# Slot writes of a gated mixture rounded one by one, its last 32 slots of an expert in plain float32 on column groups, and a rounds loop inside a branch

## The chip, the cores and the metric

One core of a Trainium2 chip runs the whole program. The metric is the device time of one execution in microseconds (us). TensorE (PE) does the matmuls, its weight loads are listed apart (PEld), VectorE is DVE, ScalarE is ACT, GpSimd is POOL, and SyncE (SP) issues most of the direct DMAs. POOL issues the indirect DMAs, which gather or scatter rows by a list of indices.

## The reference, cut to what matters

```python
def _attn_ref(r, k, v, w, u):            # B, H, S, D = 4, 8, 768, 48
    for t in range(S):
        cur = einsum('bhd,bhe->bhde', u * kt, vt)
        y[:, :, t] = einsum('bhd,bhde->bhe', rt, state + cur)
        state = wt[..., None] * state + einsum('bhd,bhe->bhde', kt, vt)

def _moe_ref(x, w1, w2, w3, w_out):      # x 3072 x 384, d_ff 1024
    return ((x @ w1) * (x @ w2) @ w3) @ w_out

def _moe2_ref(x, w_gate, w_noise, noise, w1, w2):   # 8 experts, 384 -> 1024 -> 384
    noisy = x @ w_gate + log1p(exp(x @ w_noise)) * noise
    top2 = argpartition(-noisy, 2, axis=1)[:, :2]   # softmax over the two gives top2_w
    for e in range(8):
        for k in range(2):
            mask = top2[:, k] == e
            h = maximum(x[mask] @ w1[e], 0.0)
            out[mask] += top2_w[mask, k, None] * (h @ w2[e])
```

The three run one behind the other on 3072 rows: a linear attention, a gated product with folded weights, and a mixture of 8 experts of which every row takes two.

## The kernel before, in words

**Arithmetic.** A float32 product is made of three passes: each operand is split into a high and a low part (tiles that end in h and l, type fp32r), and `mm3` (lines 170 to 172) multiplies high by high, low by high and high by low into one PSUM bank.

**First part.** After w3 and w_out are folded into the other weights, twelve groups g of 256 rows run through attention and the first mixture. A group is 12 slots of PE work (`SPG = 12`, about 2.85 us a slot), and a table `todo` hangs the other steps on slots. Two of the slots of a group carry the output of an attention chunk: line 302, 56 short float32 matmuls (32 in one chunk of four or so) with 32 columns of weights each, on the four column groups of the array in turn. ACT and DVE split its result (L308, L309).

**Gate.** For four chunks of 128 rows at a time `gate_top` finds on DVE each row's two experts, their weights (`g_sc`) and the slot of each in a table in memory (`g_sf`, float32); L623 casts all 128x8 slots to int32 (`g_si`). `gate_put` writes one column of 128 table entries of 8 bytes by an indirect DMA from POOL (L640); eight of them make a gate group. `gate_at` hangs them on slots: groups 1 to 4 on (13, 14, 17, 17, 19, 20, 23, 23) counted from the gate's own group, the fifth (`late`) on (8, 9, 9, 11, 11, 13, 13, 13). DVE keeps the order in which the program is written; the other engines are put in order by the scheduler. The sixth and last gate group is computed within the first expert's `mm1(0, ff)`, and its eight puts are written behind that loop.

**Second part.** Eight experts have 800 slots each: six tiles of 128 rows and one of 32 (`TPL`), in two halves (4 tiles, then 2 and the 32 rows). For an expert SP loads the indices from the table (`load_idx`, `ti`), POOL gathers its rows (L722, `xg`), `tr` transposes them on PE (L731), `mm1(hf, ff)` makes eight strips of the hidden rows, ACT takes their ReLU (L744), DVE the low part (L746, L748), and `mm2(e, j)` makes a tile of output, scaled by the gate weight (L762) and added to the output by a scatter from POOL (L771). The last tile (j = NT - 1, L767) multiplies a 64-column weight, 32 high and 32 low columns beside each other (`HM`), by the high and the low half of w2: 16 matmuls. L769 and L770 add its two halves. Weights come as raw float32 (`raw`, `load_e`, two loads of 768 KB for each of w1 and w2) and are split ahead of time (`split_e`; L696 ACT for the high part, L701 POOL or DVE for the low part).

**Rounds.** Should an expert get more rows than it has slots, a loop at the end, `tc.For_i(1, n)`, runs experts again. With these inputs n is 1, and its body is not run.

Of the kernel before, what the change touches and what calls it, by code (L numbers as in the profile page):

```python
# [18 lines left out]
P = 128  # L19
# [52 lines left out]
def tile_kernel(ctx: ExitStack, tc: tile.TileContext, dt, nat, w3t, wout, w1, w2, e1, e2, cf, ci, out):  # L72
# [8 lines left out]
    def f(ap):  # L81
        return ap.bitcast(F32)
# [463 lines left out]
    def gate_top(t0, n):  # L546
        def gt(shape, name, dtp=F32, bufs=1):
            return gp.tile(shape, dtp, name=name, bufs=bufs)
# [68 lines left out]
                          in1=b2[:, None, :].to_broadcast([P, n, E]), op=OP.add)  # L617
        for k in range(2):
            dve.tensor_tensor(out=M[:, :, k], in0=M[:, :, k], in1=rb, op=OP.mult)
        sf = gt([P, n, 2], "g_sf")  # L620
        dve.tensor_reduce(out=sf, in_=M, axis=mybir.AxisListType.X, op=OP.add)
        si = gt([P, n, 2], "g_si", I32, 2)
        dve.tensor_copy(out=si, in_=sf)  # L623
        GT[t0] = (si, SC)
        yield
        if last and RMAX > 1:

# [8 lines left out]
            dve.tensor_copy(out=rounds, in_=rs)  # L636

    def gate_put(t0, i, k):
        si, SC = GT[t0]
        ins = pool.indirect_dma_start(out=table, out_offset=bass.IndirectOffsetOnAxis(ap=si[:, i, k:k + 1], axis=0),  # L640
                                      in_=SC[:, i, k, :], in_offset=None)
        for p in PUT:
            tc.declare_no_dep(ins.ins, p, reason="every slot is given once")
        PUT.append(ins.ins)
# [30 lines left out]
    def open_h(pl, hf):  # L675

        n = (TA, TB)[hf] * TPT
        HH[hf] = pl.tile([P, 8, 2 * NAB[hf]], F32R, name=f"HH{hf}")
        Hh[hf], HM[hf] = HH[hf][:, :, :NAB[hf]], HH[hf][:, :, n:2 * NAB[hf] - n]
        Hl[hf] = HH[hf][:, :, 2 * NAB[hf] - n:]  # L680

    def open_b():
        EP["b"] = ctx.enter_context(tc.tile_pool(name="epb", bufs=1, side="right"))
        open_h(EP["b"], 1)

    def load_e(e, m, i):
        rw = rawp.tile([P, 1538], F32, name="raw2", tag="raw64")[:, :1536]
        sp.dma_start(out=rw, in_=(e1, e2)[m][e, :, 1536 * i:1536 * i + 1536])
        RW[e, m, i] = rw

    def split_e(e, m, i, on=pool):
        s = slice(768 * i, 768 * i + 768)
        o = 768 * (i % 2)
        src = RW[e, m, i // 2][:, o:o + 768]
        h, l = (WAh, WBh)[m][:, s], (WAl, WBl)[m][:, s]
        cast = act.copy(out=h, in_=src)  # L696
        if e == 1:

            tc.keep_in_program_order(cast)
            on = dve  # L700
        on.tensor_tensor(out=l, in0=src, in1=f(h), op=OP.subtract)  # L701
# [35 lines left out]
    def mm1(hf, ff):  # L737
        n = NAB[hf]
        s0 = hf * NAB[0]
        bank = MB[ff % (2 + hf)][:, :n]  # L740
        for kb in range(3):
            w = slice(kb * FF + ff * P, kb * FF + ff * P + P)
            mm3(bank, WAh[:, w], WAl[:, w], XT["h"][:, kb, s0:s0 + n], XT["l"][:, kb, s0:s0 + n], kb == 0, kb == 2)
        act.activation(out=Hh[hf][:, ff], in_=bank, func=AF.Relu)  # L744
        n = (TA, TB)[hf] * TPT
        dve.scalar_tensor_tensor(Hl[hf][:, ff], bank[:, :n], 0.0, f(Hh[hf][:, ff, :n]), op0=OP.max, op1=OP.subtract)  # L746
        if hf == 1:
            dve.scalar_tensor_tensor(HM[hf][:, ff, TPL:], bank[:, n:], 0.0, f(HM[hf][:, ff, :TPL]),  # L748
                                     op0=OP.max, op1=OP.subtract)

    def mm2(e, j):
        hf, jj = divmod(j, TA)
        n, s = rows_of(j), slice(TPT * jj, TPT * jj + rows_of(j))
        MC[0] ^= 1
        bank = bX[MC[0]][:, :DM]
        y = EP["a"].tile([P, DM], F32, name="ye", bufs=3)
        wt = ti(e, j)[:, 1:2].bitcast(F32)
        if j < NT - 1:
            for ff in range(8):
                w = slice(ff * DM, ff * DM + DM)  # L760
                mm3(bank[:n], Hh[hf][:, ff, s], Hl[hf][:, ff, s], WBh[:, w], WBl[:, w], ff == 0, ff == 7)
            act.activation(out=y[:n], in_=bank[:n], func=AF.Copy, scale=wt)  # L762
        else:

            for ff in range(8):
                for i, ws in enumerate((WBh, WBl)):
                    pe.matmul(bank[:2 * n], HM[hf][:, ff], ws[:, ff * DM:ff * DM + DM],  # L767
                              start=ff == 0 and i == 0, stop=ff == 7 and i == 1)
            act.activation(out=y[:n], in_=bank[:n], func=AF.Copy, scale=wt)  # L769
            dve.scalar_tensor_tensor(y[:n], bank[n:2 * n], wt, y[:n], op0=OP.mult, op1=OP.add)  # L770
        ins = pool.indirect_dma_start(out=out, out_offset=bass.IndirectOffsetOnAxis(ap=ti(e, j)[:, 0:1], axis=0),  # L771
                                      in_=y[:n], in_offset=None, compute_op=OP.add).ins

        if j == 0 or AD[0] != e:
            AD[:] = [e]
        for p in AD[1:]:
            tc.declare_no_dep(ins, p, reason="an expert's rows differ")
        AD.append(ins)
# [6 lines left out]
    def second_half(e, r, early=True):  # L785

        nx = e + 1 < E
        if nx:
            for i in range(2):
                load_e(e + 1, 0, i)  # L790
        for ff in range(8):
            mm1(1, ff)
            if ff % 2 and early:
                split_e(e, 1, 2 + ff // 4) if ff in (1, 5) else None
        for j in range(NT) if nx else (*range(NT - 2), NT - 1, NT - 2):
            mm2(e, j)
            if nx and j < 4:
                split_e(e + 1, 0, j)
            if nx and j in (4, 5):
                tr(e + 1, j - 4)  # L800
        if nx:
            for i in range(2):
                load_e(e + 1, 1, i)
# [19 lines left out]
    for t0 in range(0, NCH - GB, GB):  # L823
        late = t0 == NCH - 2 * GB
        gate_at(SPG * ((t0 + GB) // 2) + 3, t0, 1 + late,
                (8, 9, 9, 11, 11, 13, 13, 13) if late else (13, 14, 17, 17, 19, 20, 23, 23))
    at(SPG + 2, fill_table)
    for i in range(5):
        at(2 * SPG + 6 * i, fill_out, i)
# [55 lines left out]
    need(1, 1, 0)  # L885
    for ff in range(8):
        mm1(1, ff)
    for j in range(TA, NT):
        mm2(0, j)
        split_e(1, 0, j - TA)  # L890
        if j < NT - 1:
            tr(1, j - TA)
    split_e(1, 0, 3)
# [7 lines left out]
    def one_expert(e, r):  # L901
        need(e, 0, r)
        need(e, 1, r)
        for m in range(2):
            for i in range(2):
                load_e(e, m, i)
            for i in range(4):
                split_e(e, m, i)
        for hf in range(2):
            tr(e, hf)  # L910
            for ff in range(8):
                mm1(hf, ff)
        for j in range(NT):
            mm2(e, j)

    if RMAX > 1:

        n = nc.values_load(rounds[0:1, E:E + 1], min_val=1, max_val=RMAX)  # L918
        with tc.For_i(1, n) as r:
            for e in range(E):  # L920
                ne = nc.values_load(rounds[0:1, e:e + 1], min_val=1, max_val=RMAX)
                with tc.If(ne > r):
                    one_expert(e, r)


def layout(r, k, v, w, u, moe_w1, moe_w2, moe_w3, moe_w_out, moe2_w_gate, moe2_w_noise, moe2_noise, moe2_w1,
# [93 lines left out]
```

## Time and profile before

| | |
|---|---|
| three runs | 987.36, 987.98, 988.5 us; median 987.98 |
| profiled execution | 987.58 us, of which the span of the trace is 985.7 |
| PE busy | 938.5 us, 95% of the span |
| DVE, ACT, POOL busy | 444.7, 424.2, 345.3 us |
| mean granted TensorE clock | 0.984 of full speed |

The span starts with the first instruction that the profiler sees and ends with the last; 1.9 us of the time lie around it. Busy is the union of an engine's instructions.

### The profile page before, as it was taken

To read this page: it belongs to the slowest core of one execution; us is meant where nothing else is said; L and a number is where in the kernel's file an instruction comes from. 1 tells how busy PE (TensorE), PEld (TensorE's weight loads), DVE (VectorE), ACT (ScalarE), POOL (GpSimd) and SP (SyncE) were. 2 spreads that over 40 slices of the span, in tenths; PEclk is the share of its full clock that TensorE was granted. 3 is DMA by queue.
4 is the path that set the end of the run, shared out by engine and by line. 5 is a ranking of instruction groups with operands and counts; after the bars stand their busy time and mean duration, and the time that the engine had idled before them with its cause. 6 is when DMAs were issued, how large, how long until landed. Compare 5 with 4: busy or idle time off the path is not lost. (4 is left out here: it accounts for less than half of the span.)

```text
span 985.7 us, 17863 instructions
## 1 busy us (share of the span) xinstructions
PE 938.5 (95%) x7219; PEld 865.0 (88%) x7219; DVE 444.7 (45%) x1059; ACT 424.2 (43%) x879; POOL 345.3 (35%) x281
## 2 busy tenths in 40 slices
PE   7898999999999999999899999999999999999993
PEld 6787899889899899899789879899898989999893
DVE  5779666646656648646244352221303122130310
ACT  6777545445345445444252343433414343342410
POOL 2122101312401410411304635655456565544421
PEclk9999999999999999999999999999999999999997
DMA  9845975544332322410212554534254353425012
GB/s 361 344 150 188 165 174 188 134 137 152 85 110 76 108 87 76 111 52 17 81 49 81 96 154 121 122 89 74 85 109 121 89 122 91 73 85 105 11 25 29
DMA packets 49179, 111.64 MB, mean 113 GB/s; under 512 B 17600, under 2 KB 32192, under 8 KB 49088
## 3 DMA queue, kind: packets, MB, share of 16 engines
q1 hardware_dynamic: 33472, 85.98, 28.5%
q0 software_dynamic: 12160, 19.72, 11.4%
q10 hardware_dynamic: 3456, 4.72, 1.4%
q8 instruction: 58, 0.95, 0.4%
q14 instruction: 33, 0.27, 0.1%
HBM read 88.12 MB, written 22.27 MB: 112 GB/s over the span
## 5 line engine op out<-in xcount | busy, mean ns | idle before, releaser
L170 PE MATMUL pb<-XTh,WAh 128*128 128x512 f32 (+1 forms) x384 | 132.8, 347 | 1.1 <-DVE HH L748 1.0
L171 PE MATMUL pb<-XTl,WAh 128*128 128x512 f32 (+1 forms) x384 | 131.5, 343 | 0.0
L170 PE MATMUL pb<-WBh,HH 128*128 128x384 f32 x384 | 130.1, 339 | 0.9 <-ACT HH L744 0.9
L172 PE MATMUL pb<-XTh,WAl 128*128 128x512 f32 (+1 forms) x384 | 130.8, 344 | 0.0
L171 PE MATMUL pb<-WBl,HH 128*128 128x384 f32 x384 | 129.6, 338 | 0.0
L172 PE MATMUL pb<-WBh,HH 128*128 128x384 f32 x384 | 129.4, 337 | 0.0
L771 POOL DMA_INDIRECT out<-ye,ti x56 | 87.7, 1567 | 110.3 <-ACT ye L762 95.3
L746 DVE SCALAR_TENSOR_TENSOR HH<-pb,HH 128x256 fp32r<-128x256 f32 (+1 forms) x128 | 71.4, 558 | 113.5 <-ACT HH L744 110.5
L222 POOL TENSOR_TENSOR rku<-natc 128x384 f32<-128x384 f32 x24 | 26.7, 1114 | 270.0 <-DMA natc<-nat 224.8
L744 ACT ACTIVATE HH<-pb 128x288 fp32r<-128x288 f32 (+1 forms) x128 | 64.4, 505 | 124.1 <-PE pb L172 115.8
L124 DVE TENSOR_TENSOR XTl<-pb,XTh 128x512 fp32r<-128x512 f32 (+1 forms) x48 | 25.6, 571 | 162.0 <-ACT XTh L123 143.1
L762 ACT ACTIVATE ye<-pb,ti 128x384 f32<-128x384 f32 x48 | 27.9, 581 | 161.4 <-PE pb L172 117.3
L170 PE MATMUL pb<-xh,WBh 128*128 128x256 f32 x288 | 83.8, 291 | 2.9 <-DVE pp L513 2.4
L170 PE MATMUL pb<-xh,WAh 128*128 128x256 f32 x288 | 83.6, 290 | 2.8 <-ACT xh L308 2.2
L172 PE MATMUL pb<-xh,WAl 128*128 128x256 f32 x288 | 82.0, 285 | 0.8 <-DVE WAl L161 0.7
L170 PEld LDWEIGHTS pb<-XTh,WAh 128*128 128x128 f32 x384 | 72.0, 188 | 11.8 <-DVE HH L746 1.8
L172 PE MATMUL pb<-xh,WBl 128*128 128x256 f32 x288 | 81.5, 283 | 1.0 <-DVE WBl L161 1.0
L171 PE MATMUL pb<-xl,WBh 128*128 128x256 f32 x288 | 82.2, 286 | 0.0
L171 PE MATMUL pb<-xl,WAh 128*128 128x256 f32 x288 | 82.0, 285 | 0.2
L172 PEld LDWEIGHTS pb<-XTh,WAl 128*128 128x128 f32 x384 | 71.7, 188 | 8.5 <-DVE WAl L701 0.2
L171 PEld LDWEIGHTS pb<-XTl,WAh 128*128 128x128 f32 x384 | 72.1, 188 | 7.9
L722 POOL DMA_INDIRECT xg<-x_rows,ti x56 | 54.6, 975 | 66.4 <-DMA ti<-slots 34.4
(168 smaller groups left out, 2254.7 us busy)
## 6 DMA issues: line engine op xcount, KB each, us to landing
raw<-e SPq DMA_DIRECT2D x32, 768.0 KB
dtc<-dt SPq DMA_DIRECT2D x24, 772.0 KB
natc<-nat SPq DMA_DIRECT2D x24, 640.0 KB
rawf<-w3t SPq DMA_DIRECT2D x16, 512.0 KB
raw<-w SPq DMA_DIRECT2D x8, 768.0 KB
x_rows<-xo ACTq DMA_DIRECT2D x24, 192.0 KB
out<-zeros SPq DMA_DIRECT2D x4, 1152.0 KB
rawf<-wout SPq DMA_DIRECT2D x8, 384.0 KB
```

The lines of the kernel that those rows point to most:

```text
L124: (on or dve).tensor_tensor(out=l, in0=src, in1=f(h), op=OP.subtract)
L170: pe.matmul(o, wh, xh, start=start, stop=False)
L171: pe.matmul(o, wh, xl, start=False, stop=False)
L172: pe.matmul(o, wl, xh, start=False, stop=stop)
L222: pool.tensor_tensor(out=t, in0=NA[j][:, :DM], in1=NA[j][:, DM:2 * DM], op=OP.mult)
L722: pool.indirect_dma_start(out=XG[e, j][:rows_of(j)], out_offset=None, in_=x2d[:rows], in_offset=bass.IndirectOffsetOnAxis(ap=ti(e, j)[:, 0 ...
L744: act.activation(out=Hh[hf][:, ff], in_=bank, func=AF.Relu)
L746: dve.scalar_tensor_tensor(Hl[hf][:, ff], bank[:, :n], 0.0, f(Hh[hf][:, ff, :n]), op0=OP.max, op1=OP.subtract)
L762: act.activation(out=y[:n], in_=bank[:n], func=AF.Copy, scale=wt)
L771: ins = pool.indirect_dma_start(out=out, out_offset=bass.IndirectOffsetOnAxis(ap=ti(e, j)[:, 0:1], axis=0), in_=y[:n], in_offset=None, com ...
```

## The change

Three edits. L623's cast of a whole gate group is gone; `gate_put` casts its own column of 128 indices (`si[:, i, k:k + 1]`, new L639) on DVE ahead of its write, so `g_sf` has two buffers, and the late gate group's puts hang on other slots. An expert's last tile takes the hidden rows in plain float32 (`HM`, made by a new `tensor_scalar` with max), multiplies them by the raw float32 w2 on the four column groups of the array (eight matmuls, `tile_position`), adds four quarters (ACT and three DVE instructions), and stands second in the order of tiles; the raw w1 of the next expert gets buffers of its own, since raw w2 is now read until that tile. The rounds loop stands inside `tc.If(n > 1)`.

```diff
-        sf = gt([P, n, 2], "g_sf")
+        sf = gt([P, n, 2], "g_sf", bufs=2)
         dve.tensor_reduce(out=sf, in_=M, axis=mybir.AxisListType.X, op=OP.add)
-        si = gt([P, n, 2], "g_si", I32, 2)
-        dve.tensor_copy(out=si, in_=sf)
-        GT[t0] = (si, SC)
+        GT[t0] = (gt([P, n, 2], "g_si", I32, 2), sf, SC)
...
     def gate_put(t0, i, k):
-        si, SC = GT[t0]
+        si, sf, SC = GT[t0]
+
+        dve.tensor_copy(out=si[:, i, k:k + 1], in_=sf[:, i, k:k + 1])
...
-        rw = rawp.tile([P, 1538], F32, name="raw2", tag="raw64")[:, :1536]
+        if m == 0 and e:
+            rw = EP["b"].tile([P, 1536], F32, name="raww", bufs=2)
+        else:
+            rw = rawp.tile([P, 1538], F32, name="raw2", tag="raw64")[:, :1536]
...
-            dve.scalar_tensor_tensor(HM[hf][:, ff, TPL:], bank[:, n:], 0.0, f(HM[hf][:, ff, :TPL]),
-                                     op0=OP.max, op1=OP.subtract)
+            dve.tensor_scalar(HM[hf][:, ff], bank[:, n:], 0.0, None, op0=OP.max)
...
-                for i, ws in enumerate((WBh, WBl)):
-                    pe.matmul(bank[:2 * n], HM[hf][:, ff], ws[:, ff * DM:ff * DM + DM],
-                              start=ff == 0 and i == 0, stop=ff == 7 and i == 1)
+                g = ff % 4
+                pe.matmul(bank[n * g:n * g + n], HM[hf][:, ff], RW[e, 1, ff // 4][:, g * DM:g * DM + DM],
+                          start=ff < 4, stop=ff > 3, tile_position=(0, n * g))
             act.activation(out=y[:n], in_=bank[:n], func=AF.Copy, scale=wt)
-            dve.scalar_tensor_tensor(y[:n], bank[n:2 * n], wt, y[:n], op0=OP.mult, op1=OP.add)
+            for g in range(1, 4):
+                dve.scalar_tensor_tensor(y[:n], bank[n * g:n * g + n], wt, y[:n], op0=OP.mult, op1=OP.add)
...
-        for j in range(NT) if nx else (*range(NT - 2), NT - 1, NT - 2):
+        for j in (0, NT - 1, *range(1, NT - 1)):
...
-                (8, 9, 9, 11, 11, 13, 13, 13) if late else (13, 14, 17, 17, 19, 20, 23, 23))
+                (11, 11, 13, 13, 13, 14, 14, 14) if late else (13, 14, 17, 17, 19, 20, 23, 23))
...
-        with tc.For_i(1, n) as r:
-            for e in range(E):
+        with tc.If(n > 1):
+            with tc.For_i(1, n) as r:
+                for e in range(E):
```

The rows of DVE at the first gate group, the change against the kernel before: `g_sf` are the slots in float32, `g_si` in int32, `kt` and `rc` are steps of the next chunk, `am` (L247) the masked scores for its line 302.

```order
 L621 TENSOR_REDUCE g_sf<-g_M 128x8
-L623 CAST g_si<-g_sf 128x8
-L513 TENSOR_TENSOR pp<-ac,pb_67 128x512
-L247 COPY_PREDICATED am<-cit,pb_71 128x4x128
-L247 COPY_PREDICATED am<-cit,pb_72 128x4x128
+L513 TENSOR_TENSOR pp<-ac,pb_67 128x512
+L247 COPY_PREDICATED am<-cit,pb_71 128x4x128
+L247 COPY_PREDICATED am<-cit,pb_72 128x4x128
+L639 CAST g_si<-g_sf 128x1
```

The first of eight casts stands behind the two L247; the second behind the next L207, the third and fourth behind the next L309, L523 and L193, and the other four at the same places one chunk later.

The same stretch of POOL, whose order of rows was this (L222 and L223 make `rku`, a product that a later chunk needs):

```order
L640 DMA slots<-g_sc,g_si 25600x2 x8
L222 TENSOR_TENSOR rku<-natc 128x384
L223 TENSOR_TENSOR rku<-rku,cft 128x384
L222 TENSOR_TENSOR rku<-natc 128x384
L223 TENSOR_TENSOR rku<-rku,cft 128x384
```

and with the change is this:

```order
L640 DMA slots<-g_sc,g_si 25600x2 x4
L222 TENSOR_TENSOR rku<-natc 128x384
L223 TENSOR_TENSOR rku<-rku,cft 128x384
L640 DMA slots<-g_sc,g_si 25600x2 x4
L222 TENSOR_TENSOR rku<-natc 128x384
```

Eight puts in a row became four, a pair of products, and four, each put behind its own cast.

DVE at the last gate group, beside the first expert's `mm1(0, ff)` (`HH` the low part of a strip, `WBl` the low part of w2), before:

```order
L621 TENSOR_REDUCE g_sf<-g_M 128x8
L623 CAST g_si<-g_sf 128x8
L746 SCALAR_TENSOR_TENSOR HH_5758<-pb_66,HH_5758 128x512
L701 TENSOR_TENSOR WBl<-raw_5980,WBh 128x768
L629 TENSOR_TENSOR g_ct<-g_ct,pb_73 128x8
```

and with the change, the end of that stretch:

```order
L750 SCALAR_TENSOR_TENSOR HH_5784<-pb_66,HH_5784 128x512
L705 TENSOR_TENSOR WBl<-raw_6017,WBh 128x768
L750 SCALAR_TENSOR_TENSOR HH_5784<-pb_67,HH_5784 128x512
L705 TENSOR_TENSOR WBl<-raw_6017,WBh 128x768
L639 CAST g_si<-g_sf 128x1 x8
L124 TENSOR_TENSOR XTl<-pb_70,XTh 128x288
```

The index cast that stood right behind the slots' sum stands behind the fourth and last split of w2. On POOL two scatters of the first expert now stand between these eight puts and the gathers of its second half; there were none.

## Rows read from the trace of the kernel before

**Rows 1.** The profile's page: busy time, share and count of instructions by engine, and the granted TensorE clock in 40 slices of the span (in tenths).

```profile
PE 938.5 (95%) x7219; PEld 865.0 (88%) x7219; DVE 444.7 (45%) x1059; ACT 424.2 (43%) x879; POOL 345.3 (35%) x281
...
PEclk9999999999999999999999999999999999999997
```

**Rows 2.** Timeline of DVE: the first L536 copy of a group, which stands at the same place of each 12 slots (start us, us, engine, line, operation, tiles). Between 155.04 and 445.54 lie 8 groups.

```profile
155.04 0.17 DVE L536 COPY LZ<-pb 128x16 f32<-128x16 f32 x1
189.20 0.15 DVE L536 COPY LZ<-pb 128x16 f32<-128x16 f32 x1
...
229.43 0.15 DVE L536 COPY LZ<-pb 128x16 f32<-128x16 f32 x1
...
445.54 0.15 DVE L536 COPY LZ<-pb 128x16 f32<-128x16 f32 x1
484.14 0.17 DVE L536 COPY LZ<-pb 128x16 f32<-128x16 f32 x1 [0.33 <-PE pb L172]
```

**Rows 3.** Timeline of POOL: the first and the last put of the first and of the fifth gate group, each of 8 (in brackets the idle time before, and what ended it).

```profile
188.03 1.16 POOL L640 DMA_INDIRECT slots<-g_sc,g_si  x1 [1.76 <-DVE pp L513]
...
197.33 0.97 POOL L640 DMA_INDIRECT slots<-g_sc,g_si  x1 [0.30 <-issue]
...
464.52 1.18 POOL L640 DMA_INDIRECT slots<-g_sc,g_si  x1 [21.82 <-DVE g_si L623]
...
473.68 0.97 POOL L640 DMA_INDIRECT slots<-g_sc,g_si  x1 [0.30 <-issue]
```

**Rows 4.** Timeline of PE: a line 302 block with no put beside it (177.22 to 179.10), and the one beside the first gate group's puts (194.67 to 200.65).

```profile
177.22 0.28 PE L172 MATMUL pb<-xh,WBl 128*128 128x256 f32 x1
177.43 0.43 PE L302 MATMUL pb<-am,natc 128*32 128x128 f32 x8
...
177.79 0.27 PE L302 MATMUL pb<-am,natc 128*32 128x128 f32 x1
...
178.33 0.27 PE L302 MATMUL pb<-am,natc 128*32 128x128 f32 x1
...
179.10 0.19 PE L598 MATMUL pb<-g_mb,trib 128*128 128x32 bf16 x1
...
194.67 0.28 PE L172 MATMUL pb<-xh,WBl 128*128 128x256 f32 x1
194.88 0.42 PE L302 MATMUL pb<-am,natc 128*32 128x128 f32 x8
...
199.51 0.27 PE L302 MATMUL pb<-am,natc 128*32 128x128 f32 x1 [1.00 <-issue]
...
200.65 0.70 PE L170 MATMUL pb<-W0h,ph 128*128 128x400 f32 x1
```

**Rows 5.** Groups of instructions by line and form (count | busy us, mean ns | idle us of the engine before them, and what ended it): line 302 on PE.

```profile
L302 PE MATMUL pb<-am,natc 128*32 128x128 f32 x768 | 41.6, 282 | 7.5 <-issue 7.2 <-DVE am L247 0.3
```

**Rows 6.** Windows: the stretch, its length, then busy us and count of PE, PEld, DVE, ACT and POOL, granted clock, DMA share and GB/s.

```profile
200.40:204.00 3.60, 3.60 (x17) 3.36 (x12) 2.13 (x4) 3.29 (x10) 0.00 (x0) 0.53 0.51 77
467.30:480.30 13.00, 9.39 (x85) 6.99 (x84) 1.85 (x3) 1.10 (x2) 5.82 (x6) 0.87 0.03 3
522.00:533.00 11.00, 11.00 (x56) 9.77 (x55) 7.38 (x18) 2.38 (x4) 8.47 (x8) 1.00 0.28 72
600.00:960.00 360.00, 360.00 (x2045) 332.58 (x2044) 81.24 (x186) 124.31 (x224) 188.43 (x128) 1.00 0.39 90
```

**Rows 7.** Timeline of PE in the last expert: first matmul of the last tile (16 of L767), and the first behind it.

```profile
962.66 0.34 PE L767 MATMUL pb<-WBh,HH 128*64 128x384 f32 x1
...
965.45 0.34 PE L170 MATMUL pb<-WBh,HH 128*128 128x384 f32 x1
```

**Rows 8.** Groups by line and form: DVE's sum of the two halves of a last tile, one for each expert.

```profile
L770 DVE SCALAR_TENSOR_TENSOR ye<-pb,ti,ye 32x384 f32<-32x384 f32 x8 | 4.9, 608 | 48.8 <-ACT ye L769 48.8
```

**Rows 9.** Timelines about the last gate group: DVE's index cast and the fourth split of w2; POOL's first and last put of 8, and its first and third gather behind them, the three of the first expert's second half; PE's transposes of the second half (L731).

```profile
521.71 0.17 DVE L623 CAST g_si<-g_sf 128x8 int32<-128x8 f32 x1
...
529.44 0.95 DVE L701 TENSOR_TENSOR WBl<-raw,WBh 128x768 fp32r<-128x768 f32 x1
...
522.16 1.01 POOL L640 DMA_INDIRECT slots<-g_sc,g_si  x1 [34.91 <-DVE g_si L623]
...
531.79 0.97 POOL L640 DMA_INDIRECT slots<-g_sc,g_si  x1 [0.30 <-issue]
537.71 0.98 POOL L722 DMA_INDIRECT xg<-x_rows,ti  x1 [4.95 <-issue]
...
542.23 0.89 POOL L722 DMA_INDIRECT xg<-x_rows,ti  x1 [0.30 <-DMA xg<-x_rows,ti]
...
545.15 1.33 PE L731 MATMUL pb<-cft,xg 32*128 32x32 f32 x7 [1.02 <-DMA xg<-x_rows,ti]
```

**Rows 10.** Timelines behind the fifth gate group: SP's load of the first expert's indices, POOL's first and last of 4 gathers, PE's transposes of these rows.

```profile
477.16 0.33 SPq L710 DMA_DIRECT2D ti<-slots  x1
...
481.81 1.65 POOL L722 DMA_INDIRECT xg<-x_rows,ti  x1 [7.17 <-ACT WAh L696]
...
486.30 0.96 POOL L722 DMA_INDIRECT xg<-x_rows,ti  x1 [0.30 <-issue]
...
504.55 1.47 PE L731 MATMUL pb<-cft,xg 128*128 128x128 f32 x12
```

**Rows 11.** Timeline of POOL at the end: its last instruction, a scatter; the span ends at 985.7.

```profile
970.79 1.56 POOL L771 DMA_INDIRECT out<-ye,ti  x1 [2.25 <-ACTq L919]
```

More of the change, by code (lines that the diff above doesn't have):

```diff
@@ L677, in open_h @@
         n = (TA, TB)[hf] * TPT
-        HH[hf] = pl.tile([P, 8, 2 * NAB[hf]], F32R, name=f"HH{hf}")
-        Hh[hf], HM[hf] = HH[hf][:, :, :NAB[hf]], HH[hf][:, :, n:2 * NAB[hf] - n]
-        Hl[hf] = HH[hf][:, :, 2 * NAB[hf] - n:]
+        HH[hf] = pl.tile([P, 8, 2 * n], F32R, name=f"HH{hf}")
+        Hh[hf], Hl[hf] = HH[hf][:, :, :n], HH[hf][:, :, n:]
+        if hf:
+            HM[hf] = pl.tile([P, 8, TPL], F32, name="HM")
     def open_b():
@@ L743, in mm1 @@
             mm3(bank, WAh[:, w], WAl[:, w], XT["h"][:, kb, s0:s0 + n], XT["l"][:, kb, s0:s0 + n], kb == 0, kb == 2)
-        act.activation(out=Hh[hf][:, ff], in_=bank, func=AF.Relu)
         n = (TA, TB)[hf] * TPT
-        dve.scalar_tensor_tensor(Hl[hf][:, ff], bank[:, :n], 0.0, f(Hh[hf][:, ff, :n]), op0=OP.max, op1=OP.subtract)
+        act.activation(out=Hh[hf][:, ff], in_=bank[:, :n], func=AF.Relu)
+        dve.scalar_tensor_tensor(Hl[hf][:, ff], bank[:, :n], 0.0, f(Hh[hf][:, ff]), op0=OP.max, op1=OP.subtract)
         if hf == 1:
-            dve.scalar_tensor_tensor(HM[hf][:, ff, TPL:], bank[:, n:], 0.0, f(HM[hf][:, ff, :TPL]),
-                                     op0=OP.max, op1=OP.subtract)
+            dve.tensor_scalar(HM[hf][:, ff], bank[:, n:], 0.0, None, op0=OP.max)
     def mm2(e, j):
@@ L887, in tile_kernel @@
         mm1(1, ff)
-    for j in range(TA, NT):
+    for i, j in enumerate((TA, NT - 1, *range(TA + 1, NT - 1))):
         mm2(0, j)
-        split_e(1, 0, j - TA)
+        split_e(1, 0, i)
         if j < NT - 1:
@@ L912, in one_expert @@
                 mm1(hf, ff)
-        for j in range(NT):
+        for j in (0, NT - 1, *range(1, NT - 1)):
             mm2(e, j)
@@ L918, in tile_kernel @@
         n = nc.values_load(rounds[0:1, E:E + 1], min_val=1, max_val=RMAX)
-        with tc.For_i(1, n) as r:
-            for e in range(E):
-                ne = nc.values_load(rounds[0:1, e:e + 1], min_val=1, max_val=RMAX)
-                with tc.If(ne > r):
-                    one_expert(e, r)
+        with tc.If(n > 1):
+            with tc.For_i(1, n) as r:
+                for e in range(E):
+                    ne = nc.values_load(rounds[0:1, e:e + 1], min_val=1, max_val=RMAX)
+                    with tc.If(ne > r):
+                        one_expert(e, r)
 def layout(r, k, v, w, u, moe_w1, moe_w2, moe_w3, moe_w_out, moe2_w_gate, moe2_w_noise, moe2_noise, moe2_w1,
```

## The prediction

> **What bounds the kernel now.** I read the page first. PE is busy for 938.5 of 985.7 us and every other engine for less than half of that [rows 1], so only what shortens PE's work, or fills the 47 us in which it stands still, can move the end. The windows say where it stands still: not in the experts, where PE is busy for 360.00 of 360 us [rows 6], but in the first part. There a group takes 34.16 us between the same copies of two groups where nothing disturbs it (155.04 to 189.20), and 40.23 where a gate group's puts lie in it (189.20 to 229.43) [rows 2]. The timelines show the place. POOL sends eight puts back to back, 1.28 us apart, from 188.03 to 198.30 [rows 3], and line 302's 56 matmuls begin in the middle of them, at 194.88. They reach the next line at 200.65; the same block with no put beside it goes from 177.43 to 179.10 [rows 4]. The idle time is marked "issue": PE waited for nothing that the profile knows. All of line 302's idle time on its commonest form is 7.5 us, 7.2 of it "issue" [rows 5]. Behind the stall the granted clock is 0.53, so PE works for 3.6 us at nearly half speed [rows 6]. All five gate groups' puts in the first part hit a line 302 block in this way; the sixth, beside the long matmuls of the first expert (522 to 533), costs PE nothing: 11.00 of 11.00 us busy [rows 6].
>
> **A. Puts spread out.** Eight groups lie between 155.04 and 445.54: 290.5 us, against 8 x 34.16 = 273.3. The 17.2 us over are the first four gate groups' stalls with the slow clock behind them. The fifth is beside 467.3 to 480.3: PE is idle for 13.00 - 9.39 = 3.6 us, and the mean clock of 0.87 costs 0.13 x 13 = 1.7 more, 5.3 together [rows 6]. So 22.5 us is what the edit can win at the most. With the change each put follows its own cast. By the order of rows the second put stands behind L207, ahead of a line 302 block, the next two behind the L309 that reads that block's result, and so on; no more than three of a group's puts stand together, and none where PE reaches line 302. The casts themselves are seven more small DVE instructions for a gate group, of 0.17 us or less (a cast of eight columns takes 0.17 in [rows 9]); DVE is busy for 45% [rows 1], and between two casts stand instructions of the chunk on which PE waits seldom. If that cover were gone, 48 casts would cost 8 us. I leave 1 us for puts that still end near a block: **-21.5** (bounds -22.5, and -11 if half of the stalls stay).
>
> **B. The last tile.** Today its 16 matmuls go from 962.66 to 965.45: 2.79 us [rows 7]. Plain float32 on four column groups exists in line 302: there clumps of four matmuls, one for each group, follow each other five times in 0.54 us (177.79 to 178.33) [rows 4], 0.108 us for 128 columns. That is 0.85 ns for a column, 0.32 us for 384, and eight matmuls with two records each make four clumps: 1.30 us. Entering the block took 0.21 us from the matmul before it, where ordinary ones of 256 columns follow each other after 0.12 [rows 4]; about as much again at the exit gives 0.2 us. New: 1.5; saved: 1.26 for an expert, and with eight experts **-10.1** (bounds: -12 without a switch; a loss, below, if the groups don't run together). The Trainium skill, in "TensorEngine Tiling (Array Packing)", Key Properties, says that a change of the tiling mode drains TensorE. That speaks against this edit, which goes there and back once for each expert. If a drain cost a whole matmul's 0.34 us at each end, the saving would be 0.8 us, or 6 in all; the 0.21 against 0.12 here agrees with a drain, but a short one. The three sums on DVE, of 0.608 us each [rows 8], take 1.2 us more for an expert; they lie beside the following tile's 4.2 us of matmuls, in another bank, with DVE busy for 81 of 360 us [rows 6]. Without that cover they would cost 10 us. Moving the tile to second place and giving raw w1 its own buffers costs nothing as long as w2 arrives in time: its load now waits for the second tile instead of the splits, and is still some 20 us ahead of its reader, under the same full PE.
>
> **C. The rounds loop.** The last scatter begins at 970.79 and the span ends at 985.7 [rows 11]: 13 us with no work in it, in which, by the program, the scatter lands, every engine jumps over the loop's body and passes the waits at its exit, and all meet. With the branch the jump past the loop comes earlier, beside the landing of the scatter, and the waits at the loop's exit are gone. The view shows no row inside these 13 us, so I bound it: nothing at one end, a quarter of them (3.7) at the other; I take **-2.5**.
>
> **D. The last gate group.** Its index cast stood at 521.71, its puts from 522.16 to 532.76, and the gathers of the first expert's second half from 537.71, 4.95 us behind the last put; the third left at 542.23 and PE went on at 545.15, 1.02 us late, 2.9 behind that gather [rows 9]. DVE keeps the written order, and the eight casts are now written with the puts, behind the fourth split of w2, which ends at 529.44 + 0.95 = 530.4 [rows 9]. So the first put goes at 530.6, the last ends at 541.2, the gathers begin at 546.1 (two scatters that now stand ahead of them fit into the 4.95), the third leaves at 548.6, and PE goes on at 551.5. All that waits for that, transposes and `mm1(1, ff)`, is 551.5 - 545.15 = 6.3 us later, and nothing else is queued on PE for the time. **+6.5**, with bounds +4 (puts at their usual 1.28 us, part of the old wait gone elsewhere) and +9 (a slow clock behind a stall of 7 us, as in [rows 6]).
>
> **E. The late gate group.** Its puts ended at 473.68 + 0.97; the index load went 2.5 us later at 477.16, the first gather 4.65 behind that, the fourth at 486.30, and PE's transposes, at 504.55, had some 15 us to spare [rows 3, 10]. With the new slots the last three casts stand behind the copies at 484.14 and the L523 after them [rows 2], the puts end near 491.7, and by the same steps the fourth gather goes at 491.7 + 2.5 + 4.65 + 4.49 = 503.3 and lands some 3 us later, while PE wants it at 504.55. With SP's load of w2 now ahead of the index load I take **+2.6** (bounds 0 and +5).
>
> **Sum:** -21.5 - 10.1 - 2.5 + 6.5 + 2.6 = -25.0. The profiled execution took 987.6 us (span 985.7 and 1.9 around it), 0.4 under the median of the three runs: 962.6, and 963 beside the median.
>
> **The rivals.**
> - *The stalls stay.* If a line 302 block stalls whenever any put's traffic is in flight, or for something that only happens to lie there, spacing the puts out helps little, or strikes more blocks than before. For it: "issue" names no culprit. Against it: the block without a put runs undisturbed, and the stalls begin only with puts in flight. Then A is 0 and the time 987.6 - 10.1 - 2.5 + 6.5 + 2.6 = 984.
> - *The late puts cost more.* D and E both put a gather behind a chain of eight puts, a landing, an index load and three gathers, each step of which has a price of 1 to 5 us. If both fall at their upper ends and the clock drops behind them, they cost 18 instead of 9: 972. For it: the chain in D already ended last before [rows 9].
> - *They cost nothing,* because the chunk's work runs ahead by the stalls that are gone and other work fills the wait: 954. Against it: PE's order there is unchanged, and between 543.75 and the gathers' landing it has nothing else.
> - *The column groups don't run together* (the other side). If raw float32 with 384 columns runs one group after the other, eight matmuls with two records of 0.32 us take 5.2 us instead of 2.79: +2.4 for an expert, +19 in all, and the time is 987.6 - 14.9 + 19 = 992. It decides from 4.7 us for the tile on, where eight times the loss eats the other 15 us. Against it stand the clumps of four in [rows 4].
>
> **How the numbers follow.** About 0.2%, 2 us, is what a measurement of this kernel can tell from no change. Chances: forecast 0.60; stalls stay, wholly or by half, 0.13; late puts cost more 0.14; they cost nothing 0.08; column groups apart 0.05. The forecast's own range, from its terms' bounds without adding all up, is 955 to 970. The range of 952 to 978 takes in the cheap and the dear late puts and the half of the stalls, and leaves out the stalls that stay wholly, the column groups and a little below. Slower by over 2 us needs the column groups, or nearly all mishaps in A with dear late puts: 0.05. Within 2 us: 0.03. Faster: 0.92.
>
> **What would show it.** A: groups of 34.2 us each, line 302's "issue" idle near nothing, granted clock 1.00 behind the puts. B: 1.5 us between the new tile's first matmul and what follows it, and an expert 1.3 us shorter. C: under 13 us from the last scatter to the end. D and E: PE idle for some 7 us ahead of the first expert's second transposes and 2 to 3 ahead of its first, released by `xg`. The prediction is wrong if line 302 still stalls, if the new tile takes over 2 us, or if those two waits sum to over 14 us.

## The result, and the profile after

Beside four runs of the kernel before (984.67 to 988.5 us, median 987.67) the changed kernel took 963.51 to 965.62 us in four, median 964.41: a ratio of 0.9773, with a 95% interval of 0.9749 to 0.9797. The forecast was 963. Its profiled execution took 964.05 us with a span of 962.1. That gain belongs to the condition in which the kernel before needs some 988 us; in two later sittings (a sitting is a series of kernels timed side by side on one chip) it needed 966, and a close variant of the changed kernel was only 2 us faster there (the last experiment).

The page of the changed kernel (busy time by engine, and the granted clock in 40 slices):

```profile
span 962.1 us, 17805 instructions
...
PE 925.1 (96%) x7219; PEld 851.2 (88%) x7219; DVE 453.5 (47%) x1117; ACT 423.4 (44%) x879; POOL 344.4 (36%) x281
...
PEclk9998999999999999999999799999999999999997
```

PE is still the bound. Two slices are new: the 7 in the middle (529 to 553) belongs to the last gate group, and the 8 (72 to 96) lies ahead of all that the change touches.

The two profiled executions, cut at the same instructions of each (us; the groups' first L536 copies, the first L731 transposes of the third expert, the last matmul):

| stretch | before | after | difference |
|---|---|---|---|
| start to the first group's copy | 123.73 | 126.85 | +3.1 |
| nine groups, to 445.54 and 431.80 | 321.81 | 304.95 | -16.9 |
| two more, the late gate group in them, to 507.65 and 489.43 | 62.11 | 57.63 | -4.5 |
| first two experts, to 618.97 and 608.79 | 111.32 | 119.36 | +8.0 |
| to the last matmul, 969.51 and 949.57 | 350.54 | 340.78 | -9.8 |
| to the end | 16.2 | 12.5 | -3.7 |

DVE's L536 copies, which answer to [rows 2], and line 302 on PE, which answers to [rows 4] and [rows 5] (timelines, then the group of the line):

```profile
158.16 0.15 DVE L536 COPY LZ<-pb 128x16 f32<-128x16 f32 x1
192.39 0.15 DVE L536 COPY LZ<-pb 128x16 f32<-128x16 f32 x1
...
431.80 0.15 DVE L536 COPY LZ<-pb 128x16 f32<-128x16 f32 x1
463.27 0.17 DVE L536 COPY LZ<-pb 128x16 f32<-128x16 f32 x1 [0.16 <-PE pb L172]
...
197.98 0.32 PE L302 MATMUL pb<-am,natc 128*32 128x128 f32 x4
...
199.65 0.45 PE L170 MATMUL pb<-W0h,ph 128*128 128x400 f32 x1
...
L302 PE MATMUL pb<-am,natc 128*32 128x128 f32 x768 | 36.1, 276 | 0.4 <-DVE am L247 0.4
```

Eight groups take 431.80 - 158.16 = 273.6 us, 34.2 each; the block that took 5.8 us takes 1.67, and line 302's idle time marked "issue" has gone from 7.2 us to nothing.

The last tile, which answers to [rows 7], and its sums on DVE, which answer to [rows 8]:

```profile
927.22 1.50 PE L770 MATMUL pb<-raw,HM 128*32 128x384 f32 x16
928.65 0.45 PE L170 MATMUL pb<-WBh,HH 128*128 128x384 f32 x1
...
L774 DVE SCALAR_TENSOR_TENSOR ye<-pb,ti,ye 32x384 f32<-32x384 f32 x24 | 14.7, 613 | 35.2 <-ACT ye L772 34.6
```

1.43 us instead of 2.79. The last gate group, which answers to [rows 9] (DVE, POOL and PE, then windows with busy time of PE, PEld, DVE, ACT, POOL and the clock):

```profile
511.84 0.57 DVE L639 CAST g_si<-g_sf 128x1 int32<-128x1 f32 x8
...
512.26 1.01 POOL L640 DMA_INDIRECT slots<-g_sc,g_si  x1 [28.77 <-DVE g_si L639]
...
521.23 0.97 POOL L640 DMA_INDIRECT slots<-g_sc,g_si  x1 [0.30 <-issue]
...
526.99 1.01 POOL L726 DMA_INDIRECT xg<-x_rows,ti  x1 [0.96 <-issue]
...
529.58 0.87 POOL L726 DMA_INDIRECT xg<-x_rows,ti  x1 [0.30 <-issue]
...
530.32 0.48 PE L735 MATMUL pb<-cft,xg 128*128 128x128 f32 x1 [4.70 <-DMA xg<-x_rows,ti]
531.43 0.47 PE L735 MATMUL pb<-cft,xg 128*128 128x128 f32 x1 [0.64 <-DMA xg<-x_rows,ti]
532.11 2.03 PE L735 MATMUL pb<-cft,xg 32*128 32x32 f32 x7 [0.20 <-DMA xg<-x_rows,ti]
...
530.30:534.00 3.70, 2.84 (x9) 1.47 (x9) 0.71 (x2) 0.80 (x2) 2.79 (x4) 0.50 0.44 129
534.00:551.00 17.00, 16.43 (x97) 16.11 (x98) 4.75 (x18) 3.36 (x9) 7.22 (x7) 0.85 0.38 80
```

PE waits 5.5 us for the gathers, and then the granted clock falls to the lower of its two levels (1.2 GHz instead of 2.4) for a while: 0.50 of 3.7 us and 0.15 of 17 are 4.4 us of clock.

The late gate group, which answers to [rows 10], and the last scatter, which answers to [rows 11]:

```profile
476.40 0.33 SPq L714 DMA_DIRECT2D ti<-slots  x1
...
482.55 0.95 POOL L726 DMA_INDIRECT xg<-x_rows,ti  x1 [0.30 <-issue]
...
483.69 0.38 PE L735 MATMUL pb<-cft,xg 128*128 128x128 f32 x2
486.14 1.66 PE L735 MATMUL pb<-cft,xg 128*128 128x128 f32 x10 [2.07 <-DMA xg<-x_rows,ti]
...
950.85 1.55 POOL L775 DMA_INDIRECT out<-ye,ti  x1 [2.61 <-ACT ye L765]
```

The transposes that had 15 us to spare wait 2.07; from the last scatter to the end it is 11.3 us where it was 14.9.

### The profile page after: what moved, and what is told of

It reads as the page before. It is cut to its first block, busy times and chain, and to the rows that moved or that the text cites. A ratio compares the mean times of both kernels' runs of the same rounds, so it can differ in the third digit from the quotient of the medians.

```text
span 962.1 us, 17805 instructions
## 1 busy us (share of the span) xinstructions
PE 925.1 (96%) x7219; PEld 851.2 (88%) x7219; DVE 453.5 (47%) x1117; ACT 423.4 (44%) x879; POOL 344.4 (36%) x281
## 4 chain that ended last, share of the span: by engine, by line
PE 81%; issue 7%; DVE 4%; ACT 3%; DMA 2%; POOL 1%; another core or an unknown queue 1%; SPq 0%; POOLq 0%; ACTq 0%; DVEq 0%
PE pb L170 24%; PE pb L171 23%; PE pb L172 23%; PE pb L302 3%; PE pb L735 2%; PE pb L242 2%; PE pb L770 1%; PE pb L263 1%; DVE cvz L154 1%; PE pb L252 1%; DMA xg<-x_rows,ti 1%; ACT top L145 1%; DVE w3l L161 1%; DMA raw<-e 1%
## 5 line engine op out<-in xcount | busy, mean ns | idle before, releaser
L749 ACT ACTIVATE HH<-pb 128x256 fp32r<-128x256 f32 (+1 forms) x128 | 62.6, 491 | 133.0 <-PE pb L172 127.3
L640 POOL DMA_INDIRECT slots<-g_sc,g_si x48 | 50.9, 1059 | 153.7 <-DVE g_si L639 133.3
L765 ACT ACTIVATE ye<-pb,ti 128x384 f32<-128x384 f32 x48 | 27.9, 581 | 148.6 <-PE pb L172 99.4
L222 POOL TENSOR_TENSOR rku<-natc 128x384 f32<-128x384 f32 x24 | 26.8, 1116 | 173.5 <-DMA natc<-nat 144.2
```

The costliest lines, as they stand in the source:

```text
L222: pool.tensor_tensor(out=t, in0=NA[j][:, :DM], in1=NA[j][:, DM:2 * DM], op=OP.mult)
L749: act.activation(out=Hh[hf][:, ff], in_=bank[:, :n], func=AF.Relu)
```

## The experiments

In the first two sittings of experiments the kernel before took 985.21 to 995.38 us (17 runs, median 989.84) and 988.22 to 991.02 (7 runs, 989.46). "First part" is the stretch of nine groups in the table: 304.95 us with the change, 321.81 before.

**Each edit alone.** The rounding (the cast moves from `gate_top` into `gate_put`) with the late slots, on the kernel before:

```diff
-        dve.tensor_copy(out=si, in_=sf)
...
+        dve.tensor_copy(out=si[:, i, k:k + 1], in_=sf[:, i, k:k + 1])
...
-                (8, 9, 9, 11, 11, 13, 13, 13) if late else (13, 14, 17, 17, 19, 20, 23, 23))
+                (11, 11, 13, 13, 13, 14, 14, 14) if late else (13, 14, 17, 17, 19, 20, 23, 23))
```

> The kernel before with the per-slot rounding and the late group's new slots alone (the old last tile, the old loop). Theory, from the two traces: the stalls beside line 302 go (-16.9 between the same copies of groups 1 and 9, some -7 behind the late group), the late group's gathers cost +2.6, the last group's +7.8: -13 us, 974 to 975, with every line 302 block at 1.46 or 0.81 us. Rival (part of the gain in the first part comes from the other edits, through the buffers or the engines' order): less than 8 us gained, some blocks still stretched.

Measured: 978.03 us, ratio 0.9889 (0.9847 to 0.9930). The first part takes 304.92 us and every block of line 302 in it is as short as with the whole change. The edit alone brings all that the first part gains, and the waits that it adds behind take half of it back. The 974 to 975 us that were expected are missed by 3: the first two experts take 120.4 us instead of 111.3, 9.0 more and not 7.8, and the stretch ahead of the first copy is 2.7 us longer.

The last tile, on the kernel before (its matmuls, HM, the order of tiles, the buffers):

```diff
+                pe.matmul(bank[n * g:n * g + n], HM[hf][:, ff], RW[e, 1, ff // 4][:, g * DM:g * DM + DM],
+                          start=ff < 4, stop=ff > 3, tile_position=(0, n * g))
```

> The kernel before with the last tile on column groups alone. Theory: 1.1 us for each of eight experts, -9 us, 978 to 979, with the stalls beside line 302 as before. Rival of the prediction's own term: 1.26 for an expert, -10.1. Rival that the tile's move or the buffers cost elsewhere: less than 6 us gained.

Measured: 977.13 us, ratio 0.9893 (0.9851 to 0.9934), but 4.5 of that are in the first part, which this edit doesn't touch and whose stalls were a little shorter in this execution (317.33 us). The stretch to the last matmul is 340.78, as with the whole change: -9.8. The first two experts take 113.6 us instead of 111.3. (By the new order of tiles that stretch holds two last tiles, before it held one; two of 1.43 us are as long as one of 2.84, so it shows what is lost, and the next stretch what is won.) The timelines of PE and ACT and a window show why:

```profile
543.58 0.53 PE L170 MATMUL pb<-XTh,WAh 128*128 128x288 f32 x2 [2.63 <-ACT XTh L123]
...
542.66 0.58 ACT L765 ACTIVATE ye<-pb,ti 128x384 f32<-128x384 f32 x1 [6.79 <-DMA out<-ye,ti]
...
543.58:548.00 4.42, 4.42 (x20) 4.22 (x21) 1.69 (x5) 1.11 (x4) 3.62 (x3) 0.62 0.64 127
```

ACT stands at the fourth tile's output, whose buffer a scatter has to free, and behind it in ACT's queue is the cast (L123) for which PE waits. The scatter stands behind all three gathers on POOL, where before it stood ahead of the third. The wait itself adds little, since two waits of 1.0 us that the kernel before has there are gone (PE is idle for 3.65 us of the stretch, before for 3.01); behind it the granted clock is 0.62 for 4.4 us, 1.7 us lost. So the edit is worth 9.8 - 2.3 = 7.5 us, not 10.

The branch, on the kernel before:

```diff
+        with tc.If(n > 1):
             with tc.For_i(1, n) as r:
```

> The kernel before with the branch around the rounds loop alone. Theory: from the last matmul to the end 12.5 us instead of 16.2, -3.7 us, 984. Rival (the end comes at the same time whatever the loop, the 3.7 us of the changed kernel came with its other edits): 987.6, no change.

Measured: 984.24 us, ratio 0.9956 (0.9933 to 0.9978). Its last scatter starts at 970.11 and its span ends at 981.4; from the last matmul to the end it is 12.5 us instead of 16.2, all of 3.7.

```profile
970.11 1.56 POOL L771 DMA_INDIRECT out<-ye,ti  x1 [2.25 <-ACT ye L762]
```

**The last gate group rounded early.** On the changed kernel:

```diff
+        if last:
+            dve.tensor_copy(out=SI, in_=sf)
...
+        if t0 < NCH - GB:
             dve.tensor_copy(out=si[:, i, k:k + 1], in_=sf[:, i, k:k + 1])
```

> The changed kernel with the last gate group's slots cast all at once, right behind their sum as before; its puts have no casts of their own. Theory: the first expert's second transposes wait 1 us instead of 5.5 and no slow clock follows: -7 us against the changed kernel, 957. Rival (the wait comes from the two scatters that stand ahead of the gathers, or from the fourth split): the wait stays, 963 to 965.

Measured: 959.06 us, ratio 0.9703 (0.9663 to 0.9743). The puts start at 502.70, behind the sum; the transposes of the first expert's second half no longer wait for a gather; what is left there is the wait for ACT of the tile's edit (timelines of POOL and PE):

```profile
502.70 1.01 POOL L644 DMA_INDIRECT slots<-g_sc,g_si  x1 [21.36 <-DVE g_si L624]
...
524.24 1.64 PE L739 MATMUL pb<-cft,xg 128*128 128x128 f32 x9
527.98 0.85 PE L170 MATMUL pb<-XTh,WAh 128*128 128x288 f32 x2 [2.10 <-ACT ye L769]
```

The first two experts take 113.2 us instead of 119.4: the place of eight small casts in DVE's written order was worth 6.2 us. The late group's wait stays.

**The late group's old slots too.** `(8, 9, 9, 11, 11, 13, 13, 13)` with a cast each, on top of that.

> The changed kernel with the last gate group's slots cast all at once right behind their sum, and the late gate group's puts on the slots that they had before (8, 9, 9, 11, 11, 13, 13, 13) with a cast each. Theory: with two or three puts ahead of the line 302 block of slot 10 and the rest behind it the block stays at 1.46 us, the first expert's indices and gathers come some 8 us earlier, and the wait of 2.3 us ahead of its first transposes goes: 2 us under the kernel with the early cast alone. Rival (the earlier slots bring the stall back): a stretched block near 453, no gain or a loss of some 5 us.

Measured: 956.43 us, ratio 0.9661 (0.9634 to 0.9688). The first expert's transposes go in one piece, with no wait (timeline of PE):

```profile
483.84 1.47 PE L739 MATMUL pb<-cft,xg 128*128 128x128 f32 x12
```

Some of the rival came too: the block near 453 took 2.23 us from its first start to its last instead of 1.46. Against the kernel before, this version is the fastest of those here; beside the changed one it was not run in one sitting.

**What about the puts stalls PE.** Three edits of the changed kernel's first four gate groups: all eight puts on slot 15, just ahead of a line 302 block, with a cast each; the same with direct DMAs from SP in place of GpSimd's, which write the same bytes to table rows that nothing reads; and one cast and eight puts on slot 17, clear of any block (there the late group's puts stand on slot 11).

```diff
-                (11, 11, 13, 13, 13, 14, 14, 14) if late else (13, 14, 17, 17, 19, 20, 23, 23))
+                (11, 11, 13, 13, 13, 14, 14, 14) if late else (15,) * 8)
```

> The changed kernel with all eight puts of the first four gate groups on one slot, just ahead of a line 302 block, each still behind its own cast. Theory (a burst of puts beside the block is what stalls PE, however the index was rounded): the four blocks take 3 to 6 us instead of 1.46, the slow clock follows, 4 to 6 us for a group, 980 to 988. Rival (what helped was the cast by itself): blocks at 1.46, 964.

```diff
-        ins = pool.indirect_dma_start(out=table, out_offset=bass.IndirectOffsetOnAxis(ap=si[:, i, k:k + 1], axis=0),
-                                      in_=SC[:, i, k, :], in_offset=None)
+            ins = sp.dma_start(out=table[o:o + P], in_=SP2[:, i, k, :])
```

> As the one with eight puts on a slot ahead of the block, but in the first four gate groups each put is a direct DMA from SP of the same 128 pieces of 8 bytes, to table rows that are never read, so that the experts work on the table's filled-in indices for those chunks; DVE copies the 8 bytes instead of casting. Theory (GpSimd's making of the descriptors stalls PE): blocks at 1.46, about 964. Rival (the many small packets stall it): blocks stretched as with GpSimd's puts.

```diff
-        dve.tensor_copy(out=si[:, i, k:k + 1], in_=sf[:, i, k:k + 1])
+        if i == 0 and k == 0:
+            dve.tensor_copy(out=si, in_=sf)
...
-                (11, 11, 13, 13, 13, 14, 14, 14) if late else (13, 14, 17, 17, 19, 20, 23, 23))
+                (11,) * 8 if late else (17,) * 8)
```

> The changed kernel with one cast of a whole group again and its eight puts back to back, all hung on a slot just behind a line 302 block (slot 17; 11 for the late group), so that they end ahead of the next block. Theory (only the overlap with the block costs): blocks at 1.46 and 0.81, the time that of the changed kernel within 2 us. Rival (a burst costs wherever it lies in the first part): 4 us or so for a group, over 975.

Measured, in one run each: 988.45, 963.09 and 981.06 us. DVE's L536 copies at either end of eight groups, for the three in this order, and of each of GpSimd's two the row of ACT's largest wait with "remote" as its releaser in the first part (us in total, times, longest):

```profile
155.66 0.42 DVE L536 COPY LZ<-pb 128x16 f32<-128x16 f32 x2
454.16 0.15 DVE L536 COPY LZ<-pb 128x16 f32<-128x16 f32 x1
ACT xh L308 <- remote: 30.0, 4, 8.4
...
156.90 0.17 DVE L536 COPY LZ<-pb 128x16 f32<-128x16 f32 x1
431.07 0.16 DVE L536 COPY LZ<-pb 128x16 f32<-128x16 f32 x1
...
158.60 0.17 DVE L536 COPY LZ<-pb 128x16 f32<-128x16 f32 x1
448.99 0.17 DVE L536 COPY LZ<-pb 128x16 f32<-128x16 f32 x1
ACT kn L254 <- remote: 12.4, 3, 5.1
```

Eight groups take 298.5, 274.2 and 290.4 us (273.6 with the change). With a cast for each put and eight in a row the stall is back, and larger: it is not the rounding that helps. With the same bytes sent by SP (eight in 7.32 us) it is not there: it goes with GpSimd's puts. And the third kernel takes the prediction's picture down: its bursts end ahead of the blocks, the blocks beside it are not cut up, and it loses as much as the kernel before. There it is ACT that waits, up to 5.1 us, and "remote" says that the trace holds no releaser: in the burst from 203.90 to 214.55 the last of the four PE matmuls whose result L254 takes has ended by 210.75, L254 starts at 215.50, and PE stands until 216.14 (timelines of POOL, ACT and PE):

```profile
203.90 1.17 POOL L641 DMA_INDIRECT slots<-g_sc,g_si  x1 [13.12 <-DVE g_si L640]
...
213.34 1.21 POOL L641 DMA_INDIRECT slots<-g_sc,g_si  x1 [0.30 <-issue]
...
215.50 0.59 ACT L254 COPY kn<-pb 128x512 f32<-128x512 f32 x1 [5.11 <-remote]
...
210.15 0.60 PE L252 MATMUL pb<-cft,kt 128*128 128x128 f32 x4
216.14 1.10 PE L263 MATMUL pb<-natc,kn 128*64 128x48 f32 x16 [3.24 <-ACT kn L254]
```

So a long run of GpSimd's puts holds up other engines, and line 302 is only one of the places that show it. In the first burst of the kernel with puts beside the block (194.70 to 204.80) ACT stands from 197.89, when the third put has just begun, until 206.29, 1.5 us behind the last. Its row, and all the DMA queues that moved anything between 196 and 212 us:

```profile
206.29 0.48 ACT L308 CAST xh<-pb 128x384 fp32r<-128x384 f32 x1 [8.40 <-remote]
...
q1 hardware_dynamic: 792, 1.95, 40.6%
q0 software_dynamic: 256, 0.01, 1.3%
```

Two other causes fall with these rows, as far as the trace holds every packet. No packet of instructions was moved (the queues of kind `instruction` are missing), so the engines did not stand for their code. And it is no want of DMA bandwidth: the 256 packets of the puts are 0.01 MB, and from 197.6 to 205.2 all queues together moved 3 GB/s at the most. What in GpSimd's puts does it is not shown.

**Pace, length and size of the runs.** Three more kernels were to say what about a run does it: the puts off one cast with a copy on GpSimd between them, four in a row, and puts of half the entries (the other half of the table keeps its filled-in indices).

```diff
+            tc.keep_in_program_order(pool.tensor_copy(out=gp.tile([P, 384], F32, name="g_pace"), in_=cft[:, :384]))
```

> As the one with one cast for a group and its eight puts just behind a line 302 block, but with a 128x384 copy on GpSimd behind each put of the first four groups, so that the puts leave some 2.3 us apart instead of 1.28, still off one cast; the last of them now lie beside the next line 302 block. Theory (the pace of the puts is what counts): the 4.2 us that a group lost with the unpaced puts go, groups of 34 to 35 us, 963 to 967. Rival (the number of puts released at once or their nearness to a block counts): groups of 38 us or more and 975 or more.

```diff
-                (11, 11, 13, 13, 13, 14, 14, 14) if late else (13, 14, 17, 17, 19, 20, 23, 23))
+                (11, 11, 13, 13, 13, 14, 14, 14) if late else (13, 13, 13, 13, 19, 19, 19, 19))
```

> The changed kernel with the first four groups' puts on slots 13 and 19, four at a time back to back, each behind its own cast; they end ahead of the line 302 block of slot 16 or 22. Theory (the wait builds up late in a run of puts: in the burst of eight all stood still from about the sixth put to 1 us behind the last): four in a row cost little, under 1.5 us for a group, 963 to 970. Rival (every put that closely follows another costs about 0.6 us): 2 to 4 us for a group, 973 to 980.

```diff
-        ins = pool.indirect_dma_start(out=table, out_offset=bass.IndirectOffsetOnAxis(ap=si[:, i, k:k + 1], axis=0),
-                                      in_=SC[:, i, k, :], in_offset=None)
+        ins = pool.indirect_dma_start(out=table, out_offset=bass.IndirectOffsetOnAxis(ap=si[:64, i, k:k + 1], axis=0),
+                                      in_=SC[:64, i, k, :], in_offset=None)
```

> As the one with eight puts on one slot ahead of a block, but each put writes 64 of its 128 rows; the other table entries keep their filled-in indices, so the experts work on other rows. Theory (what GpSimd hands over for each put, its descriptors, builds up): at half the entries the loss of 6.2 us for a group falls by half or more, 965 to 975. Rival (the number of puts counts, whatever is in them): a loss as with whole puts, 985 or more.

Measured, in one run each: 973.19, 962.97 and 960.23 us, but in this sitting the kernel before took 966.69, also in one run. It seems that the stall was not there to be told apart, so that four in a row and half the entries are left open. The paced one lost for a reason of its own (DVE's largest wait on POOL in the first part, and its copies at either end of eight groups, 290.2 us apart):

```profile
DVE cc L229 <- POOL rku L223: 14.4, 4, 4.5
...
154.86 0.17 DVE L536 COPY LZ<-pb 128x16 f32<-128x16 f32 x1
445.08 0.18 DVE L536 COPY LZ<-pb 128x16 f32<-128x16 f32 x1
```

Eight puts and eight copies in one go stand ahead of `rku` on POOL, and DVE, then ACT and PE wait for that. DVE's four waits are 3.6 us on average, and the eight groups take 16.6 us more than with the change, some 4 for each of these four. In the changed kernel `rku` stands between two fours of puts.

**Four in a row once more**, with more runs of the kernel before beside it.

> The kernel with four puts in a row on slots 13 and 19 once more, with several runs of the kernel before beside it: the chip of the first time ran the kernel before in 966.7 us, 21 to 23 less than three others, so that nothing could be told there of a stall. Theory (a long run of puts stalls the first part, on chips on which the kernel before takes 985 us or more): on such a chip four in a row cost little, nine groups within 306 us, 961 to 968, a ratio near 0.977. Rival (every put that closely follows another costs about 0.6 us on such a chip): 2 to 4 us for a group, 973 to 980. On a chip like the last one: the kernel before again near 967, and this one within 5 us of it.

Measured: 963.62 us (961.74 to 964.67, 10 runs), and the kernel before 965.68 (962.46 to 967.51, 13 runs): ratio 0.9984 (0.9967 to 1.0). The rows of its copies give 273.6 us for eight groups:

```profile
157.86 0.17 DVE L536 COPY LZ<-pb 128x16 f32<-128x16 f32 x1
...
431.44 0.15 DVE L536 COPY LZ<-pb 128x16 f32<-128x16 f32 x1
```

So the kernel before has two levels, some 22 us apart, and keeps to one of them in all runs of a sitting: 988 to 990 in three, 966 in two. The difference is about what its stalls cost, 24, and its mean granted clock was 0.990 to 0.993 at 966 and 0.978 to 0.989 at the other level, as it would be without slow clock behind stalls. That the stalls are what is gone is argued from these two numbers: no trace of the kernel before was taken at 966. What decides it is not shown: the sitting with 989.84 and the one with 965.68 bear the same chip number. The changed kernel itself was not run in the last two sittings. This variant, which differs from it in the slots of four gate groups alone, was worth 2 us there, and that is what one would expect of the change: what the tile and the branch win, 7.5 and 3.7, is nearly what the late puts cost.

## Why the prediction was right, point by point

**A, forecast -21.5, bound -22.5: -24.0.** The copies of the eight groups came out as counted, 34.2 us each, -16.9. Behind the late group the trace shows -4.5, and the 2.6 of E are in it, so that 7.1 were won where 5.3 were counted: the idle time and the clock of the window of 467.3 to 480.3 are not all that the stall cost there. Where the other 1.8 lie is not shown. The reason given was only partly right. That PE stalled where a burst met line 302 was what the rows showed; that the meeting was needed fell with the burst that met no block. And that the stall belongs to the kernel wasn't asked at all: by the times it is there in some sittings and not in others. The 963 us stand in both, to judge by the variant with four puts in a row; the gain does not, and that it was measured where the stalls are was luck.

**B, forecast -10.1: -7.5.** The tile was sized a little too dear, 1.50 us to 1.43, so that 1.4 us are won for a tile and not 1.26 (by the prediction's own 2.79 - 1.5 it is 1.29); around it 0.2 us are lost in the other tiles and 0.1 in `mm1`, and an expert takes 56.13 us instead of 57.29, 1.16 less. Eight times that are 9.3 us. The step that failed is that the move of the tile costs nothing: the scheduler put a scatter behind a gather, ACT's queue stood for its buffer, PE stood for ACT, and the slow clock behind that took 1.7 us, once.

**C, forecast -2.5: -3.7**, with the edit alone and in the whole. That this is the upper bound to the tenth is luck: no row stood behind the bound, and 3.7 is a quarter of the 14.9 us from the scatter's start, not of the 13 that the prediction names.

**D, forecast +6.5: +6.2** by the kernel with the early cast, with the chain as written: casts at 511.84, puts from 512.26 to 522.2, the gathers behind. The puts kept 1.28 us each, and the gathers came 4.8 us behind the last one. That the size fits is in part luck. PE waits 5.5 us for the gathers where it waited 1.0, which is 4.5 more and not 6.3, and the clock takes 4.4, which the sum had left to the upper bound. Some of that hides B's loss in the same place: alone (`a_only`) D cost 9.0 us and B's move 2.3, together they are 8.0.

**E, forecast +2.6: +2.65.** From the copy of the late group to the end of its stretch it is 26.16 us (463.27 to 489.43), before 23.51 (484.14 to 507.65). Two errors cancelled in it: SP loads the indices 4.7 us behind the last put and not 2.5, and the first gather follows 2.4 us behind that and not 4.65. And it can cost more: in the kernel with the early cast and in the last one, with the same slots for these puts, the stretch took 27.9 and 27.2 us at a mean granted clock of 0.94; in the changed kernel it was 1.00.

**The sum, -25.0, met -23.6 in the traces** by some errors that cancelled (-24.0, -7.5, -3.7, +5.7 for D beside B's loss, and +2.65 make some -26.8), and by 3.1 us that belong to no term: the stretch ahead of the first copy took 126.85 us instead of 123.73, at a mean granted clock of 0.96 instead of 0.99. Over all the kernels here it lies between 123.5 and 127.3, with the same code on both sides (123.54 and 126.26 for the two with the early cast), so it is a scatter of the runs.

Of the rivals, dear late puts came in part: D and E took 12.0 us in `a_only`, where the sum has 9.1 and the rival 18. "The stalls stay" was read off the wrong thing: they went with the pacing, but in the last two sittings the kernel before was as fast without it. The column groups run together, as the clumps said.

## What to carry to other kernels

Where other engines stand without a releaser beside a run of indirect DMAs of many small entries, keep these apart on GpSimd: give each its own small index instruction, on an engine with time, so that the other engine's order paces them, and let what others wait for stand between them. When a step is moved into the issuing helper, look where the written order puts it for the last call: here eight casts behind a loop cost 6.2 us, and one cast at the old place wins them back. Time the kernel before in more than one sitting before a stall that names no releaser is counted as its own.

## What the runs showed of the hardware

A run of eight puts on GpSimd, 1.28 us apart, can hold up other engines: ACT waited up to 8.4 us, with "remote" as the releaser, and PE stood with "issue"; in the burst looked at (196 to 212 us) no packet of instructions was moved. In the last experiments the kernel before ran 22 us faster. The same entries sent by SP in a row did nothing of the kind. Switching the array to four column groups and back takes little here: 16 records of 384 columns in float32 (two for each of the eight matmuls) go from 927.22 to 928.65, 1.43 us, where four rounds at line 302's pace are 1.30, and the matmul ahead of them is 0.27 us ahead, where it was 0.17.
